# Sliding-window attention and a gated FFN on one Trainium2 core: batch 0 loaded and computed in two token halves, and every due time of the order set anew

## The chip, the cores and the metric

The kernel runs on one core of one Trainium2 chip. The metric is device time in microseconds (us), read as the median of several runs. The engines are PE (TensorE, matmul, with PEld for its weight loads), DVE (VectorE), ACT (ScalarE), POOL (GpSimd) and SP (SyncE, which here only issues transfers). SBUF is the on-chip memory of 128 partitions, PSUM the eight banks that PE writes to.

## The reference

Attention in 8 batches of 8 heads, 576 tokens, head dimension 64, each token looking 32 tokens to each side, then a feed-forward layer whose gate is a convolution over three tokens:

```python
scores = q @ k.T / 8                      # where |i - j| <= 32, else -1e9
attn = softmax(scores); x = attn @ v      # heads side by side: x is [8, 576, 512]
h = relu(x @ w_in)                        # [8, 576, 1024]
conv = conv_w[0] * h[t-1] + conv_w[1] * h[t] + conv_w[2] * h[t+1]   # per channel
out = (h * sigmoid(conv)) @ w_out         # [8, 576, 512]
```

All inputs are float32; the kernel casts to bfloat16 on the chip.

## The kernel before, in words

**Attention, per batch.** `loads(b)` brings in q and k in four transfers of 128 partitions (`qst`, `kst`: for each of q and k two groups of four heads; a partition holds 9 consecutive tokens of a head, 2304 bytes, for two pairs of heads) and v in five blocks of 128 tokens shifted by 32 (`vst`). POOL casts each to bfloat16 (`qb`, `kb`, `ve`). DVE makes a second copy of v shifted by 64 tokens (`vo`, `shift`). `transposes` (line 479) turns q and k on PE, ACT and DVE copy the result to `qT` and `kT`. `scores` (line 509) works on a pair of heads: PE multiplies 64 queries by the 128 keys around them, ACT takes the exponential in two parts (five and four query blocks), and DVE multiplies by the 0/1 `mask`. `values` (line 537) multiplies by `ve` and `vo`, whose 65th column of ones gives the sum; DVE takes its reciprocal (`rec`) and writes the normalised `xn`. `x_turned` (line 578) turns `xn` on PE, and ACT or DVE copy it to `xT`, the input of the FFN.

**FFN.** Two batches, 1152 tokens, make three chunks of 384 tokens, 12 chunks in all. `first` (line 615) multiplies by `w_in`, one of eight blocks m of 128 channels at a time, and ACT or DVE take the relu into `hT`. `gates` (line 705) does the convolution as 32x32 matmuls with diagonal weights (`diag_w`) for four blocks, ACT takes a tanh (`tn`), DVE forms the product (`gT`). Since the convolution's result comes out turned by 32 partitions per block, `moves` (line 688) turns `hT` the same way by transfers (`gT<-hT`), and the rows of w_out are loaded turned. `second` (line 758) multiplies by `w_out`, and the copy to `wst` is stored. Chunk 0 needs batch 0 alone, chunk 1 the end of batch 0 and the start of batch 1, so chunk 1 of the first two batches is done in two parts: part 0 is its half in batch 0, part 1 the one in batch 1. Chunk 2 lies in batch 1.

**Who sets the order.** Nothing is issued while the code above runs. Each step is a task with its engines, an estimated duration, what it reads and writes, and a due time t; `Order.run` (line 65) then plays a list schedule: at each step the engine that can start first takes, among its ready tasks, the one with the least t. The instructions are issued in the order found and each engine keeps to it, so an instruction that waits holds up everything behind it on its engine. The due times come from the numbers in `PARAMS` (line 832): start times of the chunks, the distance of the pairs, offsets for each kind of step. Loads of batches 0 and 1 are due long before time 0, in the order batch 0, w_in (two halves of 1 MB through `wst`), batch 1, w_out. All these transfers go through SP's one queue; a load waits until the casts have emptied its staging tile, and further until the queue has room. The staging tiles for q, k and v exist once; the cast tiles exist for two batches, the `attn` tiles for four pairs.

Lines of the profile: nearly all work is issued through a helper (line 274), so the rows below tell instructions by their tiles.

Of the kernel before, what the change touches and what calls it, by code (L numbers as in the profile page):

```python
# [31 lines left out]
class Order:  # L32
# [3 lines left out]
    def __init__(self):  # L36
        self.tasks, self.writer, self.readers = [], {}, {}

    def add(self, kinds, emit, t, reads=(), writes=(), opens=None, ps=(), after=(), claims=()):


        deps = set(after)
# [10 lines left out]
        task = Task(len(self.tasks), kinds, emit, t, deps, opens, ps)  # L53
        task.soft = soft - deps
        for k in reads:
            self.readers.setdefault(k, []).append(task)
# [8 lines left out]
    def run(self, emit=True):  # L65
        free = {"PE": 0.0, "ACT": 2800.0, "DVE": 6000.0, "POOL": 4400.0, "SP": 800.0}
# [128 lines left out]
def kernel(  # L195
# [152 lines left out]

    def loads(b):
        i = b % NLD  # L350

        def load_qk(y, j):
            src = (q, k)[y][b, 4 * j:4 * j + 4, :, :]
            sync.dma_start(
                qkst[y][j].rearrange("p e j d -> p e (j d)"),
                bass.AP(src.tensor, src.offset, [[RP * D, 128], [2 * S * D, 2], [1, RP * D]]),
            )

# [21 lines left out]
        if b < 2:  # L380
            x, dx = (-100.0 if b == 0 else -50.0), 0.1
        else:
            x, dx = t0 - PARAMS["LD"], Q["LX"]
# [5 lines left out]

        for j in range(NPH):  # L390
            for y in range(2):
                t = x + n * dx
                o.add({"SP": dma(256, 110)}, lambda e, y=y, j=j: load_qk(y, j), t,
                      writes=[("st", y, j)], after=paced())
                before.append(o.tasks[-1])
                o.add({"POOL": pl(1152)}, lambda e, y=y, j=j: cast_qk(y, j, e), t,
                      reads=[("st", y, j)], writes=[("b", i, y, j)])
                n += 1
        for c in range(NBLK):
            t = x + n * dx  # L400
            o.add({"SP": dma(1024, 21)}, lambda e, c=c: load_v(c), t, writes=[("vst", c)], after=paced())
            before.append(o.tasks[-1])
            o.add({"POOL": pl(512)}, lambda e, c=c: cast_v(c, e), t,
                  reads=[("vst", c)], writes=[("ve", i, c)])
            n += 1
        for cs in ((0, 2), (2, 4)) if b == 0 else ((0, 4),):
            for half in range(2):
                o.add({"DVE": dve(520 * (cs[1] - cs[0]), 4)},
                      lambda e, cs=cs, half=half: shift(half, cs), x + n * dx,
                      reads=[("ve", i, c + half) for c in range(*cs)],  # L410
                      writes=[("vo", i, c, half) for c in range(*cs)])

    def load_w_in():
        for h in range(2):
# [9 lines left out]
            o.add({"SP": dma(512, 95)}, load, -60.0, writes=[("ws", 4 * h + c) for c in range(4)])  # L424
            for c in range(KC):
                o.add({"POOL": pl(512)}, lambda e, h=h, c=c: cast(e, h, c), -60.0 + h,
                      reads=[("ws", 4 * h + c)], writes=[("w_in", h, c)])

    def load_w_out():
        rows = moe_w_out.rearrange("(h c p) f -> p h c f", c=4, p=128)  # L430
        for c in range(4):
            def load(e, c=c):
                for lo, at, n in turn(c):
# [5 lines left out]
            o.add({"SP": dma(256, 95, len(turn(c)))}, load, -40.0,  # L439
                  writes=[("ws", 4 * h + c) for h in range(2)])  # L440
            for h in range(2):
                o.add({"POOL": pl(512)}, lambda e, h=h, c=c: copy(e, w_out_sb[:, 4 * h + c, :], ws[:, 4 * h + c, :]),
# [18 lines left out]
    def conv_weights():  # L461
        ps = Banks(1)
        o.add({"PE": pe(200.0, "f32")},
              lambda e: tensor.matmul(bank(ps, 0)[:, 0:3 * MB], conv_w24, ident24, start=True, stop=True),
              5.0, opens=ps, writes=[("cw24",)])
        o.add({"DVE": dve(24)}, lambda e: vector.tensor_copy(
            out=conv_w_sb.rearrange("p k m -> p (k m)"), in_=bank(ps, 0)[:, 0:3 * MB]),
            5.0, reads=[("cw24",)], writes=[("cw",)], ps=[ps])
        o.add({"DVE": dve(768)}, lambda e: vector.tensor_tensor(
# [5 lines left out]
    def transposes(g2):  # L475
# [3 lines left out]
        i, n = b % NLD, g2 % NKT  # L479
        for y in range(2):  # L480
# [16 lines left out]
            o.add({"PE": pe(280.0, "rows")}, mm, t + Q["TR"],  # L497
                  reads=[("b", i, y, j)], writes=[("tr", g2, y)], opens=ps,
                  claims=[("T", n, y, h) for h in range(2)])
            for h in range(2):  # L500
                o.add({"ACT": act(576), "DVE": dve(576)},
                      lambda e, ps=ps, h=h, to=to: copy(
                          e, to[:, h, :, :], half(ps, h).rearrange("p (j x) -> p x j", x=64)),
                      t + Q["TC"], reads=[("tr", g2, y)], writes=[("T", n, y, h)], ps=[ps])
# [4 lines left out]
    def scores(g):  # L509
# [3 lines left out]
        for part, ts in enumerate((range(0, 5), range(5, 9))):  # L513
            ps = Banks(2, 2)
            w = 64 * len(ts)

            def mm(e, ps=ps, ts=ts):
                for x in ts:
# [8 lines left out]
            o.add({"PE": pe(28.0 * len(ts), "rows")}, mm, t + Q["SC"] * d,  # L527
                  reads=[("T", n, y_, y) for y_ in range(2)],
                  writes=[("sc", g, part)], opens=ps, claims=[("a", a, part)])
            o.add({"ACT": act(2 * w)},  # L530
# [3 lines left out]
                  t + Q["EX"] * d, reads=[("sc", g, part)], writes=[("a", a, part)], ps=[ps])  # L534
        o.add({"DVE": (850.0, 850.0, None)},
# [3 lines left out]
    def values(g):  # L539
# [5 lines left out]
        ps = Banks(2, 2)  # L545

        def mm(e):
            for h in range(2):
                for c in range(NBLK):
                    for j in range(2):  # L550
                        x = min(2 * c + j, NT - 1)
                        tensor.matmul(
                            bank(ps, h)[64 * j:64 * j + 64, 65 * c:65 * c + 65],
# [6 lines left out]
        o.add({"PE": pe(29.0 * 10, "cols")}, mm, t + Q["AV"] * d,  # L560
              reads=[("a", a, 0), ("a", a, 1)] + [("ve", i, c) for c in range(NBLK)]
              + [("vo", i, c, h) for c in range(NBLK - 1) for h in range(2)],
              writes=[("av", g)], opens=ps, claims=[("xn", b % 2, pr), ("rec", a)])

        def po():
            return pair(ps, 0)[:, :, 0:65 * NBLK].rearrange("p e (c x) -> p e c x", x=65)
# [301 lines left out]
```

## Time and profile before

| | us |
|---|---|
| median of 3 runs (lowest, highest) | 241.77 (241.15, 247.62) |
| the profiled execution's own time | 243.37 |
| its span in the trace | 241.7 |
| PE busy | 208.1 |
| ACT busy | 164.0 |
| DVE busy | 160.1 |
| POOL busy | 80.9 |

The span is what the trace covers, from the first instruction to the last; the profiled execution's time has 1.67 us more, which lie outside it. A row of the timeline gives start, length, engine, line, operation, destination and source tile with their shapes, how many instructions are merged in it, and in brackets how long the engine had been idle before and what ended that. The forty digits of a row of the page are slices of 6.04 us: busy share in tenths, or the granted clock of PE in tenths of full speed.

### The profile page before, as it was taken

Reading aid. Unit: us, or ns where it says so; the run is one execution under the profiler, and the core shown is the slowest. Engines: PE = TensorE matmul, PEld = TensorE weight load, DVE = VectorE, ACT = ScalarE, POOL = GpSimd, SP = SyncE. Lnnn points to the kernel's source line nnn. Section 1 sums busy time; section 2 is a strip of 40 time slices with the busy share of each in tenths; the row PEclk is TensorE's granted clock in tenths of the full one; section 3 lists DMA queues with packets and bytes.
Section 4 is the critical chain, followed back from the end, with each engine's and each line's share of the span. In section 5 each row is a group of like instructions: output and inputs, shape, how many; then the busy total and the mean of one; then the engine's idle time right before and its main releaser. Section 6 shows DMA issues by size and latency. Waiting matters only on the chain. (4 is left out here: it accounts for less than half of the span.)

```text
span 241.7 us, 9128 instructions
## 1 busy us (share of the span) xinstructions
PE 208.1 (86%) x3878; PEld 124.3 (51%) x3906; DVE 160.1 (66%) x268; ACT 164.0 (68%) x291; POOL 80.9 (33%) x96
## 2 busy tenths in 40 slices
PE   1536995589998869999999998999999999999993
PEld 0425464365655454565455654655555655555541
DVE  7586166998575899546399779698684595524140
ACT  1650586445698576679977886679778885876751
POOL 5757744536613444662236517321000000000000
PEclk9999999758999997999999999999999999999999
DMA  6999999989698899969489989756132223342534
GB/s 237 292 289 392 248 233 223 275 229 337 168 290 186 217 293 355 328 186 278 98 207 356 264 225 281 161 129 205 37 129 55 79 105 68 123 110 54 177 113 181
DMA packets 67228, 49.62 MB, mean 205 GB/s; under 512 B 46172, under 2 KB 52340, under 8 KB 67188
## 3 DMA queue, kind: packets, MB, share of 16 engines
q1 hardware_dynamic: 67152, 49.03, 71.6%
q8 instruction: 30, 0.49, 0.9%
q14 instruction: 10, 0.08, 0.1%
q10 hardware_dynamic: 36, 0.01, 0.0%
HBM read 32.52 MB, written 9.44 MB: 174 GB/s over the span
## 5 line engine op out<-in xcount | busy, mean ns | idle before, releaser
L274 PE MATMUL pst<-xT,w_in_sb 128*128 128x385 bf16 (+2 forms) x416 | 75.4, 322 | 1.6 <-ACT xT L274 0.6
L274 PE MATMUL pst<-w_out_sb,gT 128*128 128x512 bf16 x260 | 64.3, 384 | 3.2 <-issue 2.2
L274 PEld LDWEIGHTS <-w_in_sb 128*128 128x128 bf16 x416 | 37.6, 100 | 25.8 <-issue 3.4
L274 ACT ACTIVATE hT<-pst 128x385 bf16<-128x385 f32 (+2 forms) x80 | 38.6, 489 | 11.1 <-PE pst L274 10.1
L274 DVE SCALAR_TENSOR_TENSOR gT<-tn,gT 128x384 bf16<-128x384 f32 (+2 forms) x52 | 42.4, 842 | 3.9 <-DMA gT<-hT 3.9
L274 POOL CAST ve<-vst 128x512 bf16<-128x512 f32 x40 | 29.4, 741 | 45.7 <-DMA vst<-in_v_dram 43.5
L274 ACT ACTIVATE attn<-pst 128x640 bf16<-128x640 f32 x64 | 39.4, 667 | 4.9 <-PE pst L274 4.9
L274 PEld LDWEIGHTS <-gT 128*128 128x128 bf16 x288 | 26.6, 99 | 31.0 <-issue 3.3
L274 ACT ACTIVATE tn<-pst 128x768 f32<-128x768 f32 (+1 forms) x52 | 37.4, 768 | 6.5 <-PE pst L274 4.6
L274 ACT COPY wst<-pst 128x512 f32<-128x512 f32 x36 | 21.2, 588 | 29.6 <-PE pst L274 28.1
L274 DVE TENSOR_TENSOR attn<-attn,mask 128x1152 bf16<-128x1152 bf16 x32 | 26.9, 846 | 12.3 <-ACT attn L274 12.1
L274 DVE TENSOR_TENSOR xn<-pst,rec 128x640 bf16<-128x640 f32 x32 | 25.8, 818 | 0.5
L274 DVE SCALAR_TENSOR_TENSOR gT<-tn,hT 128x384 bf16<-128x384 f32 (+1 forms) x26 | 14.7, 564 | 16.5 <-ACT tn L274 16.4
L274 POOL CAST qb<-qst 128x1152 bf16<-128x1152 f32 x16 | 19.9, 1242 | 16.2 <-DMA qst<-in_q_dram 12.5
L274 POOL CAST kb<-kst 128x1152 bf16<-128x1152 f32 x16 | 19.9, 1243 | 16.0 <-DMA kst<-in_k_dram 14.3
L274 PE MATMUL pst<-hT,diag_w 32*32 32x384 bf16 (+1 forms) x1248 | 21.2, 322 | 1.8 <-DVE xn L274 1.0
L274 ACT COPY xT<-pst 128x1024 bf16<-128x1024 bf16 (+1 forms) x16 | 11.8, 781 | 13.9 <-PE pst L274 13.9
L274 PEld LDWEIGHTS <-attn 128*64 128x64 bf16 x640 | 14.1, 119 | 13.6 <-issue 8.6
L274 PE MATMUL pst<-ve,attn 128*64 128x65 bf16 x384 | 17.4, 206 | 3.8 <-DVE attn L274 2.3
L274 PE MATMUL pst<-qT,kT 64*128 64x64 bf16 x576 | 17.5, 197 | 3.1 <-DVE kT L274 0.8
L274 PE MATMUL pst<-vo,attn 128*64 128x65 bf16 x256 | 15.6, 206 | 3.3 <-DVE vo L274 3.3
L274 PEld LDWEIGHTS <-kT 64*128 64x128 bf16 x576 | 12.2, 98 | 12.0 <-issue 9.2
(37 smaller groups left out, 163.4 us busy)
## 6 DMA issues: line engine op xcount, KB each, us to landing
qst<-in_q_dram SPq DMA_DIRECT2D x16, 576.0 KB, 6.4
kst<-in_k_dram SPq DMA_DIRECT2D x16, 576.0 KB, 7.3
out_dram<-wst SPq DMA_DIRECT2D x11, 768.0 KB, 5.8
vst<-in_v_dram SPq DMA_DIRECT2D x24, 256.0 KB, 5.5
vst<-in_v_dram SPq DMA_DIRECT2D x16, 192.0 KB, 5.9
wst<-in_moe_w_in_dram SPq DMA_DIRECT2D x2, 1024.0 KB, 7.9
gT<-hT SPq DMA_DIRECT2D x14, 144.0 KB, 3.6
gT<-hT SPq DMA_DIRECT2D x34, 48.0 KB, 2.1
```

Source lines behind the costliest of these rows:

```text
L274: return lambda *args, **kwargs: fixed(do(*args, **kwargs))
```

## The change

Batch 0 is split in two halves by tokens in q and k (tokens 0 to 287 and 288 to 575). Each half load of q or k is two transfers of 64 partitions (32 rows by two heads, the rows outermost); the first halves of k are issued on ACT's queue, all others on SP's. Each half is cast, turned, scored, masked and multiplied with v by itself: the scores in query blocks 0 to 3 and 4 to 8, the values in token blocks 0, 1 and 2 to 4. Transposes of batch 0 are 64x64 in place of 64x128. `load_w_in` takes one half at a time and stands behind the half of batch 0; its casts may go to ACT as well as to POOL. All loads of batches 0 and 1, w_in and w_out are tied to one another in a line, in the order in which they are added. Chunk 0's `first` is done in two halves of 193 and 192 columns; its `gates`, `moves` and `second` are as before. Each task gets a name and an index, `NUDGE` adds an offset to its due time, and `PARAMS` has new values. Two estimates of the planner differ: ACT is counted free from 5400 ns on, not 2800, and the copy of `xT` on DVE at twice the rate. Batches 1 to 7 have the same instructions as before, in another order.

```diff
+    def add(self, name, kinds, emit, t, ..., claims=(), sub=0, line=None):
+        index = self.index + 20 * sub
+        t += self.nudge.get(name, {}).get(index, 0.0)
...
+        if line:
+            soft.add(line[-1])
+        if line is not None:
+            line.append(task)
...
-        free = {"PE": 0.0, "ACT": 2800.0, "DVE": 6000.0, "POOL": 4400.0, "SP": 800.0}
+        free = {"PE": 0.0, "ACT": 5400.0, "DVE": 6000.0, "POOL": 4400.0, "SP": 800.0}
...
+        def load_half(y, j, half):
+            for e_ in range(2):
+                src = (q, k)[y][b, 4 * j + 2 * e_:4 * j + 2 * e_ + 2, 32 * RP * half:32 * RP * half + 32 * RP, :]
+                (scalar if y and not half else sync).dma_start(
+                    qkst[y][j][64 * e_:64 * e_ + 64, half, :, :].rearrange("p j d -> p (j d)"),
+                    bass.AP(src.tensor, src.offset, [[RP * D, 32], [S * D, 2], [1, RP * D]]),
+                )
...
+        if b == 0:
+            for half in range(2):
+                t = x + 3.0 * half
+                for j in range(NPH):
+                    for y in range(2):
+                        o.add("qk", ..., load_half(y, j, half), t, writes=[("st0", y, j, half)], sub=half, line=lead)
+                        o.add("qc", {"POOL": pl(576)}, ..., cast_half(y, j, half, e), t, ...)
+                        t += 0.1
+                for c in (range(0, 3), range(3, NBLK))[half]:
+                    v_block(c, t)
+                    t += 0.1
+                v_shift((2 * half, 2 * half + 2), t)
+                load_w_in(half, t + 1.0)
+            return
...
-                o.add({"POOL": pl(512)}, lambda e, h=h, c=c: cast(e, h, c), -60.0 + h,
-                      reads=[("ws", 4 * h + c)], writes=[("w_in", h, c)])
+                o.add("wic", {"POOL": pl(512), "ACT": act(512)}, lambda e, h=h, c=c: cast(e, h, c), t,
+                      reads=[("ws", 4 * h + c)], writes=[("w_in", h, c)], sub=h)
...
+        if b == 0:
+            for half in range(2):
+                for y in range(2):
+                    transposes_half(g2, y, half, t + Q["B0"] * half)
+            return
...
-        for part, ts in enumerate((range(0, 5), range(5, 9))):
+        for part, ts in enumerate((range(0, 4), range(4, 9)) if first_ else (range(0, 5), range(5, 9))):
...
+            if first_:
+                lo = 64 * ts[0]
+                o.add("mk", ..., attn[:, :, lo:lo + w] * mask[:, :, lo:lo + w], ...)
...
+        cs = range(NBLK) if part is None else (range(0, 2), range(2, NBLK))[part]
...
+        if c == 0:
+            for m in range(MB):
+                first(c, m, 0, T0 + Q["A0"] + m * 0.5)
...
-                    first(c, m, part, t + m * dt)
+                    first(c, m, part if c else 1, t + m * dt)
...
-        for i in range(NP):
-            values(b * NP + i)
+        for part in (0, 1) if b == 0 else (None,):
+            for i in range(NP):
+                values(b * NP + i, part)
...
-PARAMS = {"P": 23.98, "T0": 17.65, "T1": 35.65, "T2": 7.73, "B1": 27.27, "LD": 15, "LEAD": 0,
-          "EARLY": 2.48, "MV": 2000.0, "C1": 8.2, "PY": 6, "TR": -5.1, "TC": -10, "SC": -0.08,
...
+PARAMS = {"P": 26.5, "T0": 10, "T1": 34.66, "T2": 16, "B1": 22.98, "LD": 21.05, "LEAD": 6.54,
+          "EARLY": 6.11, "MV": 2000.0, "C1": 7.98, "PY": 5.59, "TR": -1.75, "TC": -7.8,
...
+NUDGE = {
+    "qk": {0: 50.82, 1: -13.88, 2: 12.29, 3: -10.82, 4: 21.55, 5: 73.01, 6: 1.84, 7: 16.51,
+        20: 21.78},
...
```

More of the change, by code (lines that the diff above doesn't have):

```diff
@@ L380, in loads @@
         if b < 2:
[L381 removed]
+            x, dx = -100.0, 0.1
         else:
@@ L525, in mm @@
                         )
[L527 to L530, printed above, removed]
+            o.add("sc", {"PE": pe(28.0 * len(ts), "rows")}, mm, t + Q["SC"] * d,
+                  reads=need, writes=[("sc", g, part)], opens=ps, claims=into,
+                  sub=part if first_ else 0)
+            o.add("ex", {"ACT": act(2 * w)},
                   lambda e, ps=ps, ts=ts, w=w: scalar.activation(
```

216 lines of the change are left out of this document (144 added, 72 removed), and 72 rows, old and new, of tables (NUDGE, PARAMS).

## Prediction

> **What bounds the kernel now.** I read the page first: the span, the busy times, the forty slices.
>
> ```profile
> span 241.7 us, 9128 instructions
> ...
> PE 208.1 (86%) x3878; PEld 124.3 (51%) x3906; DVE 160.1 (66%) x268; ACT 164.0 (68%) x291; POOL 80.9 (33%) x96
> PE   1536995589998869999999998999999999999993
> ...
> PEclk9999999758999997999999999999999999999999
> ```
>
> TensorE (PE) carries the kernel: 208.1 us of 241.7, so 33.6 us idle, most of it in the first ten slices of 6 us. Next I asked for the busy times by stage. The columns behind the window are its length, then busy us of PE, PEld, DVE, ACT and POOL, granted clock, share of the DMA engines and GB/s.
>
> ```profile
> 0.00:12.00 12.00, 4.09 (x110) 3.59 (x110) 7.91 (x26) 4.91 (x8) 7.64 (x13) 1.00 0.93 265
> 12.00:25.50 13.50, 6.74 (x142) 5.24 (x136) 9.84 (x18) 4.67 (x8) 9.76 (x15) 1.00 1.07 344
> 25.50:36.00 10.50, 10.46 (x183) 6.31 (x184) 3.70 (x8) 7.05 (x13) 5.88 (x8) 1.00 0.99 223
> 36.00:49.80 13.80, 7.33 (x228) 5.58 (x205) 11.48 (x21) 6.83 (x13) 6.67 (x9) 0.84 0.94 236
> 49.80:55.60 5.80, 5.80 (x125) 4.07 (x126) 4.99 (x10) 3.66 (x6) 2.48 (x3) 0.50 0.93 289
> 55.60:70.00 14.40, 13.88 (x285) 8.65 (x286) 10.73 (x16) 10.03 (x22) 7.88 (x8) 1.00 0.87 252
> 70.00:90.00 20.00, 16.09 (x400) 10.09 (x401) 16.38 (x26) 15.73 (x28) 7.82 (x10) 0.99 0.92 236
> ...
> 96.00:230.00 134.00, 130.24 (x2333) 74.13 (x2352) 86.96 (x139) 103.09 (x184) 30.36 (x32) 1.00 0.59 166
> 230.00:241.70 11.70, 7.82 (x81) 3.52 (x80) 2.24 (x4) 4.44 (x7) 0.00 (x0) 1.00 0.40 148
> ```
>
> Three stretches matter. To 25.5 PE lacks 14.7 us while the DMA engines are full (0.93, 1.07). From 36 to 49.8 it lacks 6.5 us, and after that it is full but at half clock: 5.8 us that do the work of 2.9. From 70 to 90 it lacks 3.9 us. From 96 to 230 only 3.8 us of 134 are idle, and the 3.9 us after 230 are the tail of the last rows. So the time is set by when PE gets its full supply, and that is when batch 1's attention has been turned: chunks 2 and up need it. The timeline shows the stations to that point (start, length, engine, operation, and the wait before it).
>
> ```profile
> 4.76 1.14 POOL L274 CAST qb<-qst 128x1152 bf16<-128x1152 f32 x1 [1.65 <-DMA qst<-in_q_dram]
> ...
> 10.15 1.15 POOL L274 CAST kb<-kst 128x1152 bf16<-128x1152 f32 x1 [0.78 <-DMA kst<-in_k_dram]
> ...
> 15.14 0.79 POOL L274 CAST ve<-vst 128x512 bf16<-128x512 f32 x1 [0.47 <-DMA vst<-in_v_dram]
> 16.49 0.99 POOL L274 CAST ve<-vst 128x512 bf16<-128x512 f32 x1 [0.56 <-DMA vst<-in_v_dram]
> 18.90 2.29 POOL L274 CAST w_in_sb<-wst 128x512 bf16<-128x512 f32 x4 [1.43 <-DMA wst<-in_moe_w_in_dram]
> 21.63 2.29 POOL L274 CAST w_in_sb<-wst 128x512 bf16<-128x512 f32 x4 [0.44 <-DMA wst<-in_moe_w_in_dram]
> 23.86 1.15 POOL L274 CAST qb<-qst 128x1152 bf16<-128x1152 f32 x1
> ...
> 28.58 1.15 POOL L274 CAST kb<-kst 128x1152 bf16<-128x1152 f32 x1 [0.81 <-DMA kst<-in_k_dram]
> ...
> 34.57 0.62 POOL L274 CAST ve<-vst 128x512 bf16<-128x512 f32 x1 [1.53 <-DMA vst<-in_v_dram]
> ```
>
> POOL waits for a DMA before nearly every cast: the loads set the pace. Batch 0's four q and k loads arrive 1.8 us apart ((10.15 − 4.76) / 3), a block of v every 1.35 us, half of w_in in 2.73 us. The last block of batch 1's v is cast at 35.2.
>
> ```profile
> 36.11 0.76 DVE L274 TENSOR_TENSOR attn<-attn,mask 128x1152 bf16<-128x1152 bf16 x1
> 36.85 0.76 DVE L274 COPY qT<-pst 128x576 bf16<-128x576 bf16 x1
> 39.45 0.76 DVE L274 COPY kT<-pst 128x576 bf16<-128x576 bf16 x1 [1.84 <-PE pst L274]
> 40.23 1.03 DVE L274 COPY vo<-ve 64x2080 bf16<-64x2080 bf16 x1
> ...
> 42.16 1.11 DVE L274 COPY vo<-ve 64x2080 bf16<-64x2080 bf16 x1
> ...
> 44.28 0.21 DVE L274 RECIPROCAL rec<-pst 128x10 f32<-128x10 f32 x1
> ...
> 48.90 0.82 DVE L274 TENSOR_TENSOR xn<-pst,rec 128x640 bf16<-128x640 f32 x1
> ```
>
> Though v was there at 35.2, VectorE (DVE) shifts it only at 40.23: it stands behind a copy of kT, which waits for PE. The shift ends at 43.27, the last xn at 49.72. **This chain of 14.5 us behind the last load is what I expect to shrink.**
>
> **The change part by part.**
>
> *Loads.* The same bytes in another order: half 0 of q and k, v blocks 0 to 2, half of w_in, then the second halves, then batch 1. By the rates above: the first halves of q and k are in at about 6.5 (3.6 us for four half loads, the first some 0.9 us sooner than 4.76), v 0 to 2 at 10.3, w_in's first half at 13.0, the second halves at 16.6, v 3 and 4 at 19.3, the rest of w_in at 22.0. That was 21.63, so batch 1 comes as before and its last v at about 35. Eight more issues on SP at 0.46 us (12 in place of 4) cost nothing while the queue is full. Four go to ACT, at the 0.65 us of its own first one (row below): 0.80 + 5 × 0.65 = 4.05, before ACT's table load at 5.07. A 64-partition load has no row; its rate lies between the 295 KB in 0.9 us taken here and half of that, which would add 7.2 us for all four and both halves; I take no loss, since the nearest rows, the 128-partition loads, move the same pieces of 2304 bytes. With the whole 7.2 the sum below would come to 241.
>
> ```profile
> 0.80 0.65 ACTq L305 DMA_DIRECT2D conv_w<-in_moe_conv_w_dram  x1
> ...
> 0.80 0.44 SPq L274 DMA_DIRECT2D qst<-in_q_dram  x1
> ...
> 1.30 0.46 SPq L274 DMA_DIRECT2D kst<-in_k_dram  x1
> ...
> 5.07 1.28 ACT L274 ACT_TABLE_LOAD   x1 [5.07 <-DVE conv_w_sb L274]
> ...
> 5.96 0.66 PE L274 MATMUL pst<-ident,qb 64*128 64x64 bf16 x18 [2.14 <-POOL qb L274]
> ```
>
> The Trainium skill (Perfetto Trace Analysis, DMA Optimizations) says splitting transfers lets some start sooner if the DMA engines are generally idle. Here they are not (0.93, 1.07), and by that rule the split brings nothing: the time would be the first rival's below.
>
> *Added work in batch 0.* PE: 72 more transposes at 0.66 / 18 us, 2.6 us; DVE: four masks, four reciprocals, four xn more. A half costs more than half: relu takes 0.56 us for 385 columns and 0.36 for 193 (rows below), so 0.16 is fixed, and 12 × 0.16 = 1.9 us. Chunk 0's relus, 16 in place of 8, add 8 × 0.16 = 1.3 on ACT and DVE. POOL's casts add about 4 × 0.1. All of it falls before 25.5, where PE has 6.8 us free from 12 on, DVE 3.7, ACT 8.8, POOL 3.7: costed at 0. If that cover were gone, DVE's 1.9 would be paid; that is the other end.
>
> ```profile
> 32.67 0.56 DVE L274 TENSOR_SCALAR hT<-pst 128x385 bf16<-128x385 f32 x1 [1.08 <-ACT tn L274]
> ...
> 34.64 0.36 DVE L274 TENSOR_SCALAR hT<-pst 128x193 bf16<-128x193 f32 x1 [0.68 <-PE pst L274]
> ```
>
> *Chunk 0's first half earlier.* Its input needs only tokens 0 to 255 and w_in's first half, so four of its eight blocks can run from about 16 on, all eight from about 23. Until now its first weight load came at 25.51, and PE was then full to 36 (10.46 us of 10.5), so batch 1's transposes and scores were mixed in late and DVE waited for the kT copy till 39.45. Weight loads of that stretch show the pace:
>
> ```profile
> 25.51 0.14 PEld L274 LDWEIGHTS <-w_in_sb 128*128 128x128 bf16 x2 [0.68 <-POOL qb L274]
> ...
> 27.74 0.15 PEld L274 LDWEIGHTS <-w_in_sb 128*128 128x128 bf16 x1 [0.17 <-issue]
> 28.06 1.20 PEld L274 LDWEIGHTS <-w_in_sb 128*128 128x128 bf16 x7 [0.17 <-issue]
> ```
>
> One per 0.32 us up to 28.06, then about 0.16: PE is at half speed until then, though the granted clock reads 1.00. Half of chunk 0 is 32 matmuls, 5.1 us at half speed, that leave the full stretch for the idle one.
>
> *Batch 1's chain.* With 5.1 us off PE and w_in's casts allowed on ACT too (POOL's last four, 2.29 us, are what the cast at 23.86 follows without a wait), the transposes of batch 1 can be copied before v is in. Then the shift starts at 35.2, ends after 1.03 + 1.11 at 37.3, and the chain of the four pairs follows. Before, that took 49.72 − 43.27 = 6.45 with three masks in it; without them four times (0.21 + 0.82) = 4.1. So the last xn ends between 41.4 and 43.8, 8.3 to 5.9 us earlier. No gain is the other bound, if DVE is again busy with something else. I take the cautious row, 5.9, call it 6: what is late next is DVE, with chunk 0's products. PE has 6.5 us idle there to absorb the shift.
>
> *Clock after 45.* Half clock from 49.8 to 55.6 costs 2.9 us. The stretch before will again be a thin one, so I count 0; −2.9 is the bound.
>
> *New targets everywhere.* Every priority is another, so every later wait can go or grow. What can go: 0.5 + 3.9 + 3.8 idle after 55.6 without the tail, 8.2. What can come: the gap of 70 to 90 once more, 3.9. Between −8.2 and +3.9 the middle is −2.2; I take −2.
>
> **Sum.** 241.7 − 6 − 2 = 233.7 us of span. The profiled execution took 243.37 us, 1.67 beyond its span; the median of the runs is 241.77, 1.60 below it, as long as the span. In the runs' measure: 241.77 − 8 = **233.8 us**.
>
> **The rivals.**
>
> *Nothing moves (241).* The loads end as before, DVE is in demand from 36 to 49.8 (11.48 of 13.8), and half 1 of batch 0 is later by 2.8 us (v at 19.3 for 16.49). If DVE takes products and masks ahead of the shift, the 14.5 us stay. Price: the start gains 0, and the later part keeps between nothing and half of its 2: 241. For it: the full DMA. Against: v lay there unused for 5 us. With what the targets may do, between 238 and 244. The Trainium skill's rule on splitting (Perfetto Trace Analysis, DMA Optimizations) ends in this case.
>
> *PE stays fed (227).* The last xn at 41.4 (−8.3), no half clock (−2.9) and −3.5 of the later idle: 241.8 − 14.7 = 227.1. For it: idle DVE from 25.5 to 36 (3.70 of 10.5). Against: the loads still leave PE little to do till 35.
>
> *Slower (248).* DVE becomes the bound from 70 to 96. It is busy 16.38 of 20 there, and batch 3's shift, masks and xn go through it while PE waits. If the targets put products before them, as they did in 36 to 49.8, each pair adds a mask and a wait, and PE drops to half clock. It decides when the new idle time there passes the 8 us gained; 5 us more, and the kernel is slower by over 2%. Price: a second gap like 36 to 55.6 (6.5 + 2.9) and batch 1's gain lost, less 3 us of the rest: 241.8 + 9.4 − 3 = 248. Against: PE is at 97% from 96 on, under the same priority rule.
>
> **How the numbers follow.** About 2% is what measurement can tell from no change: below 236.9 is faster, above 246.6 slower. Forecast 0.58, for which I give 229 to 237; PE fed 0.12; nothing moves 0.20; slower 0.10. Faster 0.70, same 0.20, slower 0.10. The range goes from the fed case to the top of the unmoved one: 227 to 243; outside lie the slower case and bits of two others.
>
> **What would show it.** Right: a matmul of chunk 0 with 193 columns before 22; the last v cast of batch 1 near 35; the shift of v within a us of it; the last xn of batch 1 by 44; PE full from 45 on. Wrong: v's last cast after 38 (the half loads are slow); the shift late again (DVE order); more than 8 us of idle PE between 55 and 96 (targets); relus or masks of batch 0 still running at 26 (the added work was not covered).

## The result, and the profile after

The kernel before took 241.67 us (median, 241.15 to 247.62), the changed one 250.23 us (247.15 to 250.98): a ratio of 1.032, with a 95% interval of 1.022 to 1.041. It is slower, where the forecast was 3% faster, and it lies outside the forecast's range. The profile shown is of a run of 247.15 us, and that of before of one of 243.37, so of the 8.6 us between the medians they can show only the part that their spans have, 245.4 − 241.7 = 3.7 us. Here and below medians are over all runs of a kernel and ratios over its runs in the faster of the chip's two states, so the two need not agree.

First the page of the changed kernel (span, busy times, TensorE's slices of 6.1 us, granted clock), then its busy times in the windows shown of before.

```profile
span 245.4 us, 9371 instructions
...
PE 209.9 (86%) x3984; PEld 128.8 (52%) x4010; DVE 163.8 (67%) x289; ACT 159.8 (65%) x294; POOL 79.5 (32%) x96
PE   1658787357998978989999799999999999999994
...
PEclk9999799655999999999999999999999999999999
```

```profile
0.00:12.00 12.00, 4.31 (x106) 3.61 (x106) 4.95 (x24) 4.91 (x8) 6.89 (x15) 1.00 0.92 201
12.00:25.50 13.50, 8.52 (x196) 6.77 (x192) 8.53 (x22) 7.87 (x16) 6.26 (x11) 1.00 1.09 314
25.50:36.00 10.50, 9.23 (x133) 8.07 (x134) 4.69 (x14) 6.26 (x16) 7.38 (x9) 0.84 1.04 262
36.00:49.80 13.80, 7.62 (x246) 5.82 (x243) 8.06 (x14) 8.74 (x16) 7.04 (x11) 0.81 1.05 278
49.80:55.60 5.80, 3.16 (x116) 2.52 (x117) 5.43 (x10) 1.60 (x4) 3.32 (x3) 0.50 0.85 228
55.60:70.00 14.40, 12.93 (x206) 8.22 (x207) 9.16 (x17) 6.77 (x16) 7.62 (x8) 0.79 0.71 212
...
96.00:230.00 134.00, 129.55 (x2334) 74.50 (x2353) 100.71 (x156) 96.55 (x175) 33.15 (x34) 1.00 0.65 173
230.00:245.40 15.40, 11.71 (x98) 5.15 (x97) 3.37 (x6) 5.87 (x10) 0.00 (x0) 1.00 0.44 164
```

To 25.5 us PE is busy 2.0 us longer than before (4.31 + 8.52 against 4.09 + 6.74). From 25.5 to 49.8 it is busy 0.9 us less (9.23 + 7.62 against 10.46 + 7.33). Behind 96 the rows are alike: 129.55 of 134 against 130.24, and a tail with 3.7 us idle against 3.9. The largest difference lies at 48 to 60, of which these are the rows, first of before, then of after with the 12 us ahead of it:

```profile
48.00:60.00 12.00, 11.05 (x203) 7.20 (x204) 11.03 (x18) 5.79 (x11) 6.26 (x6) 0.68 0.94 279
```

```profile
36.00:48.00 12.00, 6.17 (x214) 4.80 (x213) 6.26 (x12) 7.46 (x14) 6.59 (x10) 0.85 1.06 270
48.00:60.00 12.00, 7.60 (x213) 5.28 (x215) 11.63 (x20) 4.75 (x9) 6.54 (x5) 0.50 0.95 286
```

I call lost time a window's idle PE time plus its busy time multiplied by one minus the clock. Before, these 12 us lose 0.95 + 11.05 × 0.32 = 4.5; after, 4.4 + 7.60 × 0.50 = 8.2. The difference, 3.7 us, is as large as that of the spans. The other windows differ too, but come to about nothing together: the changed kernel loses 2.0 us less to 25.5, 2.7 more from 25.5 to 36 and 2.4 less from 72 to 96. From 48 to 60 PE is at half clock and waits, while DVE is busy 11.63 of 12.

Two timelines of the changed kernel show what came late: first batch 0's second half and chunk 0, then batch 1.

```profile
5.38 1.14 POOL L283 CAST qb<-qst 128x576 bf16<-128x576 f32 x1 [2.27 <-DMA qst<-in_q_dram]
...
16.77 0.67 POOL L283 CAST qb<-qst 128x576 bf16<-128x576 f32 x1 [0.98 <-DMA qst<-in_q_dram]
...
18.44 2.50 PE L283 MATMUL pst<-xT,w_in_sb 128*128 128x193 bf16 x16 [0.17 <-DVE xT L283]
...
20.11 0.67 POOL L283 CAST kb<-kst 128x576 bf16<-128x576 f32 x1 [0.48 <-DMA kst<-in_k_dram]
...
24.20 2.12 DVE L283 TENSOR_TENSOR attn<-attn,mask 128x640 bf16<-128x640 bf16 x3
...
27.04 1.44 DVE L283 TENSOR_TENSOR xn<-pst,rec 128x384 bf16<-128x384 f32 x3
...
31.04 0.69 DVE L283 COPY xT<-pst 128x1024 bf16<-128x1024 bf16 x1 [1.89 <-PE pst L283]
31.79 1.42 PE L283 MATMUL pst<-xT,w_in_sb 128*128 128x193 bf16 x15 [0.41 <-DVE xT L283]
```

```profile
36.55 0.62 POOL L283 CAST ve<-vst 128x512 bf16<-128x512 f32 x1 [0.29 <-DMA vst<-in_v_dram]
...
40.83 1.12 DVE L283 COPY vo<-ve 64x2080 bf16<-64x2080 bf16 x1
...
46.55 0.50 PE L283 MATMUL pst<-ident,kb 64*128 64x64 bf16 x12 [3.91 <-issue]
47.13 0.76 DVE L283 COPY kT<-pst 128x576 bf16<-128x576 bf16 x1 [3.56 <-PE pst L283]
...
54.04 1.01 DVE L283 SCALAR_TENSOR_TENSOR gT<-tn,gT 128x384 bf16<-128x384 f32 x2
55.10 0.75 DVE L283 TENSOR_TENSOR xn<-pst,rec 128x640 bf16<-128x640 f32 x1
55.78 1.95 DVE L283 SCALAR_TENSOR_TENSOR gT<-tn,gT 128x768 bf16<-128x768 f32 x2
57.66 0.81 DVE L283 TENSOR_TENSOR xn<-pst,rec 128x640 bf16<-128x640 f32 x1
```

Chunk 0's first matmuls start at 18.44, as intended. But the second half's last cast of k starts at 20.11, and from there transposes, scores, exponentials, four masks, values, four xn and a turn follow one another until its x is copied at 31.73. Before, all of batch 0 had been turned and chunk 0 had begun at 25.51; now chunk 0's second half, mixed with chunk 1's part in batch 0, runs from 31.79 to 38.7. Batch 1's last k of the second group is then copied only from 47.13, behind a stop of PE, and its xn stand between chunk 0's products. The last xn ends at 58.47; before, 49.72; forecast, 43.8.

The ends of DVE's last copies of xT for batches 1, 2 and 3 are the stations I use from here on (ACT's last copies end at most 0.4 us later). Before:

```profile
54.25 0.28 DVE L274 COPY xT<-pst 128x256 bf16<-128x256 bf16 x1
93.20 0.28 DVE L274 COPY xT<-pst 128x256 bf16<-128x256 bf16 x1
107.16 0.69 DVE L274 COPY xT<-pst 128x1024 bf16<-128x1024 bf16 x1 [2.08 <-PE pst L274]
```

After:

```profile
62.35 1.46 DVE L283 COPY xT<-pst 128x1024 bf16<-128x1024 bf16 x2 [0.71 <-PE pst L283]
95.49 1.27 DVE L283 COPY xT<-pst 128x1024 bf16<-128x1024 bf16 x2
111.77 1.29 DVE L283 COPY xT<-pst 128x1024 bf16<-128x1024 bf16 x2 [1.97 <-PE pst L283]
```

That is 54.5, 93.5 and 107.9 against 63.8, 96.8 and 113.1: 9.3, 3.3 and 5.2 us later, and 3.7 later at the end.

### The profile page after: what moved, and what is told of

It is laid out like the page before. It is cut to its first block, busy times and chain, and to the rows that moved or that the text cites. A ratio compares the mean times of both kernels' runs of the same rounds, so it can differ in the third digit from the quotient of the medians.

```text
span 245.4 us, 9371 instructions
## 1 busy us (share of the span) xinstructions
PE 209.9 (86%) x3984; PEld 128.8 (52%) x4010; DVE 163.8 (67%) x289; ACT 159.8 (65%) x294; POOL 79.5 (32%) x96
## 4 chain that ended last, share of the span: by engine, by line
PE 58%; DMA 14%; DVE 11%; ACT 7%; issue 4%; SPq 2%; POOL 1%; ACTq 0%; DVEq 0%; POOLq 0%
PE pst L283 58%; DMA kst<-in_k_dram 5%; ACT attn L283 4%; DMA wst<-in_moe_w_out_dram 3%; DVE gT L283 3%; DVE xn L283 3%; DMA vst<-in_v_dram 3%; DMA qst<-in_q_dram 2%; DVE attn L283 2%; DMA gT<-hT 2%; SPq L283 2%; ACT tn L283 1%; DVE vo L283 1%; DVE hT L283 1%; ACT hT L283 1%
## 5 line engine op out<-in xcount | busy, mean ns | idle before, releaser
L283 PE MATMUL pst<-xT,w_in_sb 128*128 128x385 bf16 (+3 forms) x448 | 73.7, 312 | 1.4 <-DVE xT L283 0.7
L283 PEld LDWEIGHTS <-w_in_sb 128*128 128x128 bf16 x448 | 40.8, 100 | 22.4 <-issue 2.8
L283 ACT ACTIVATE hT<-pst 128x385 bf16<-128x385 f32 (+3 forms) x88 | 39.4, 462 | 13.8 <-PE pst L283 13.0
L283 ACT ACTIVATE attn<-pst 128x640 bf16<-128x640 f32 (+1 forms) x64 | 38.8, 662 | 5.6 <-PE pst L283 5.2
L283 DVE TENSOR_TENSOR attn<-attn,mask 128x1152 bf16<-128x1152 bf16 (+2 forms) x36 | 29.8, 835 | 11.2 <-ACT attn L283 10.7
L283 POOL CAST qb<-qst 128x1152 bf16<-128x1152 f32 (+1 forms) x18 | 20.8, 1157 | 26.1 <-DMA qst<-in_q_dram 22.4
L283 DVE TENSOR_SCALAR hT<-pst 128x385 bf16<-128x385 f32 (+3 forms) x24 | 11.6, 485 | 24.8 <-PE pst L283 16.6
L283 POOL CAST kb<-kst 128x1152 bf16<-128x1152 f32 (+1 forms) x18 | 19.2, 1068 | 23.4 <-DMA kst<-in_k_dram 15.2
L283 DVE TENSOR_TENSOR xn<-pst,rec 128x640 bf16<-128x640 f32 (+2 forms) x36 | 26.1, 738 | 0.5
L283 PEld LDWEIGHTS <-attn 128*64 128x64 bf16 x640 | 14.1, 119 | 16.4 <-issue 9.5
L283 ACT COPY qT<-pst 128x576 bf16<-128x576 bf16 x23 | 14.6, 655 | 7.6 <-PE pst L283 7.6
```

What stands on the lines that cost most here:

```text
L283: return lambda *args, **kwargs: fixed(do(*args, **kwargs))
```

## The experiments

**What they have to tell apart.** Theory A: the split itself, with half 1's chain of eleven us, makes the start late. Theory B: the new due times do it, and the split would have paid with the old ones. Theory C: the half loads are slow, or their queue is. Theory D: the loss is not in the start but in the order behind it. All ratios are to the kernel before, run on the same chip, with 95% intervals.

**The change's halves one at a time.** `targets_alone` loads and computes batch 0 whole and keeps the new due times and the planner's estimates. `split_old_targets` keeps the split with the old due times.

```diff
-        if b == 0:
+        if b == 0 and SPLIT:
...
+SPLIT = False
```

> Batch 0 and chunk 0 whole as before, loads and w_in in the order of before, w_in's casts on POOL alone; due times, offsets and planner estimates of the changed kernel. Theory H (batch 0's second half comes late, and all behind it): about as before, 239 to 243, the first block of batch 0's x turned near 21.5 and all of it by 25. Theory T (the new due times make an order that the chip runs badly): 247 or more, with the last xn of batch 1 after 55 as in the changed kernel.

Measured: 250.39 us, 1.024 (1.010 to 1.037). The due times alone cost 2.4%, without any split and with the old transfers; the forecast had them at −2 us. Batch 0's x is turned by 26.1 here (25 expected, 25.4 before), but batch 1's only by 59.5 (54.5 before).

```diff
-PARAMS = {"P": 26.5, "T0": 10, "T1": 34.66, "T2": 16, "B1": 22.98, "LD": 21.05, "LEAD": 6.54,
+PARAMS = {"P": 23.98, "T0": 17.65, "T1": 35.65, "T2": 7.73, "B1": 27.27, "LD": 15, "LEAD": 0,
...
-NUDGE = {
...
+NUDGE = {}
```

> The split in halves and the load order of the change, with the due times of before and no offsets. Theory H: still slow, 245 to 250, the last block of batch 0's x turned near 31 as in the changed kernel. Theory T: 242 or less, the last xn of batch 1 before 52.

Measured: 246.96 us (242.02 to 249.52) beside 243.17 (240.72 to 245.32) of the kernel before, with no usable interval. No gain shows with the old due times either, but whether there is a loss can't be read from this run; `halves_old_start` below asks again.

**The loads.** `w_in_behind` puts both halves of w_in behind batch 0's second half; `no_w_out_load` is the changed kernel, in its order, without the 2 MB of w_out.

```diff
-                load_w_in(half, t + 1.0)
+            for half in range(2):
+                load_w_in(half, x + 3.0 * half + (1.7 if half == 0 else 1.6))
```

> The changed kernel with one edit: both halves of w_in load behind batch 0's second half, not one between. Theory H: the last cast of batch 0's k comes 2.7 us earlier (near 18, not 20.1), x is turned 2 to 3 us earlier, and the time falls by 2 to 4 us to about 246. Theory T: no change beyond 1.5 us, unless the order happens to come out otherwise.

Measured: 261.86 us, 1.081 (1.071 to 1.091). The second half of k was cast from 17.61, 2.5 us sooner than in the changed kernel, but x was turned only by 30.2 and the last xn came at 59.2. It settles nothing: with other loads the planner put the whole kernel into another order, so the 8% can't be laid to the loads.

```diff
-                for lo, at, n in turn(c):
+                for lo, at, n in ():
```

> The changed kernel with w_out never loaded (its casts take what lies in the staging tile, so the second matmul uses other weights); the order of instructions is the same. Theory S (the 3.9 us in which PE stands in the midst of a row of transposes is an instruction fetch that waits behind full DMA engines, and the half clock follows from it): the stop at 42.6 shrinks below 1 us and the time falls by 4 to 7 us. Theory H: the stop may go, but the time falls by 2 us at most, since batch 0's half sets the start.

Measured: 246.35 us, 1.011 (0.999 to 1.023), two points less than the change. PE's stop is gone, and from 36 to 48 PE does 8.99 us where it did 6.17 in the changed kernel:

```profile
36.00:48.00 12.00, 8.99 (x283) 7.30 (x280) 8.19 (x15) 10.78 (x22) 7.11 (x11) 0.93 0.57 162
```

The same edit in the kernel before (`before_no_w_out`) tells whose cost it is.

> The kernel before without the load of w_out (its casts take what lies in the staging tile). The order is unchanged. If PE's stop of 2.2 us at 37 is a fetch behind full DMA engines, it goes here too, and the time falls by 2 to 4 us, near what no_w_out_load gained on the change (2.1 points): then the stop is no cost of the change by itself. If the time falls by under 1 us, the longer stop is a cost of the change.

Measured: 240.29 us, 0.993 (0.989 to 0.997). Without the load the change is still slower, 1.011 against 0.993, by 1.8%. The other 1.4 points of its 3.2% would then be that load's. This is an estimate: the interval of 1.011 alone goes from 0.999 to 1.023, and without the load not only the stop is gone, the DMA engines have less to do as well (a share of 0.57 from 36 to 48, in place of 1.06).

`whole_loads` brings both halves of q and k with the first transfers, in the order of the changed kernel; `whole_b1` is that with batch 1 put first as below; `k_on_sp` takes the k halves off ACT's queue.

```diff
-            for e_ in range(2):
-                src = (q, k)[y][b, 4 * j + 2 * e_:4 * j + 2 * e_ + 2, 32 * RP * half:32 * RP * half + 32 * RP, :]
+            for e_ in range(0 if half else 2):
+                src = (q, k)[y][b, 4 * j + 2 * e_:4 * j + 2 * e_ + 2, :, :]
```

> The changed kernel with the same order of instructions, but each first-half transfer of q and k brings both halves (64 partitions, two pieces of 2304 bytes each) and the second-half transfers are gone. Theory H: batch 0's second half is cast by 13, its x turned by 25 in place of 31, and the time falls by 4 us or more. Theory D: batch 0 may be earlier, but batch 1's last xn stays after 54 and the time falls by 2 us at most.

Measured: 254.56 us, 1.047 (1.038 to 1.056), and `whole_b1` 257.41 us, 1.061 (1.055 to 1.067). POOL keeps its order, so the second half's casts still wait behind v and w_in while everything else comes later: a miss, which says only that the kept order is made for the half loads.

```diff
-                (scalar if y and not half else sync).dma_start(
+                sync.dma_start(
```

> The changed kernel, its order unchanged, with the first halves of k issued on SP like all others. If ACT's queue slows the first loads (four q halves took SP 2.86 us, 0.72 each, where 0.46 was the rule): the first casts come 0.5 to 1 us earlier and the time falls by up to 2 us. If the queue does not matter: no change within 1.5 us, perhaps slower by the issues that SP now makes in a row.

Measured: 250.69 us, 1.034 (1.026 to 1.042): the queue makes no difference to the time. The first cast does come sooner (4.51 for 5.38), and batch 1's last v is cast 3.3 us later than in the changed kernel (by 40.51 for 37.17); in this order that costs nothing the runs can show.

**Batch 1 first.** If the end hangs on batch 1, its steps have only to be put ahead of all others. `b1_first` does that in the changed kernel, `before_b1_first` in the one before.

```diff
+for _n in ("tr", "tc", "sc", "ex", "mk", "av", "rc", "xm", "xt", "xc"):
+    for _i in ((1, 21, 41) if _n in ("xt", "xc") else (1,)):
+        NUDGE[_n][_i] = -100.0
```

> The changed kernel with one edit: batch 1's transposes, copies, scores, exponents, masks, values, xn and its turning get an offset of -100 us, so that each engine takes them before anything else that is ready. Theory D (the new due times let DVE do gate products and relus between batch 1's four pairs, so x of batch 1 comes late): the last xn of batch 1 ends by 50 in place of 58.5, PE is full from about 52, and the time falls by 5 us or more, to 245 or less. Theory H (batch 0's second half comes late): the last xn moves by 3 us at most, and the time stays above 247.

> The kernel before with the offset of -100 us on the same steps of batch 1, nothing of the split. Theory D: in the kernel before the chain stood behind other work too (the shift of v 5 us late), so the last xn moves from 49.7 to 46 or less and the time falls by up to 3 us, to 239. Theory H says nothing of it: 240 to 244.

Measured: 254.07 us, 1.045 (1.034 to 1.055), and 244.4 us, 1.009 (1.003 to 1.014). In both the last xn of batch 1 came sooner (52.9 and 47.2 us, against 58.47 and 49.72), and neither is faster than the kernel that it was made from. That was the first sign against the forecast's premise. But both were ordered anew to the end.

**Start and rest apart.** So in the next kernels each step is given the place that it has in another kernel's plan: the steps of batches 0 and 1 and chunks 0 to 2 ("start") from one kernel, all later ones ("rest") from another. The list schedule still decides ties and delays, so of the 230 pairs of neighbouring steps on PE in the rest 14 to 43 are other ones than in the plan that the rest is taken from (53 and 55 in `halves_whole_loads` and `b1_first_old_rest`, below).

```diff
+            if x.key in RANK:
+                e, x.t = RANK[x.key]
+                x.kinds = {e: x.kinds[e]}
```

> The changed kernel's start (loads and attention of batches 0 and 1, weights, chunks 0 to 2) in its order, and from batch 2 and chunk 3 on the order of the kernel before: each step is given the engine and the planned time that it had there as its due time. Theory S (the loss is made in the start): 247 to 250, as slow as the change. Theory R (the order of the rest is at fault): 242 to 244, about as before.

> The split in halves, with the due times and estimates of before in the start too; the rest in the order of before. It tells the split from the new due times. Theory S with the split at fault (batch 0's second half late): 245 or more, the last xn of batch 1 after 53. Theory S with the due times at fault: 243 or less, the last xn by 51.

> Batch 0 whole as before, the start ordered by the new due times, the rest in the order of before. Theory S with the due times at fault: 246 or more. Theory S with the split at fault, or theory R: 244 or less.

> The kernel before in its own order up to batch 1 and chunk 2, and the order of the changed kernel from batch 2 and chunk 3 on. Theory R: 246 or more. Theory S: 240 to 243, and where the rest of the new order is better, as its planner counts, 238.

| start | due times in it | rest | us | ratio (95%) |
|---|---|---|---|---|
| halves | new | old | 251.12 | 1.038 (1.031 to 1.045) |
| halves | old | old | 249.23 | 1.022 (1.014 to 1.029) |
| whole | new | old | 253.48 | 1.044 (1.038 to 1.051) |
| whole | old | new | 243.82 | 1.007 (1.003 to 1.011) |

D falls: the new rest behind the old start costs 0.7%. A, taken as the split together with its loads, and B are both right: each by itself is enough (2.2% and 4.4%), and they don't add.

`halves_whole_loads` keeps the halves in the computation, with old due times and old rest, but loads each q and k of batch 0 whole, with v and then w_in behind them, in the order of before. One thing is not as before: the transfers are still pairs of 64 partitions, where the kernel before has one of 128.

```diff
-                        o.add("qk", ..., t, writes=[("st0", y, j, half)], sub=half, line=lead)
+                        if not half:
+                            o.add("qk", ..., t, writes=[("st0", y, j, h) for h in range(2)], sub=half, line=lead)
```

> Batch 0 computed in halves, with due times and estimates of before, but loaded as before: each of q and k whole, both halves in one pair of transfers, then v, then w_in; the rest in the order of before (from batch 2 and chunk 3 on). To be held against halves_old_start (1.0215). If the transfers in halves and their order are what the split costs: 244 or less, x of batch 0 turned by 26. If computing in halves costs: 247 or more.

Measured: 250.31 us, 1.037 (1.031 to 1.042). x of batch 0 is turned by 30.8 (25.4 before). But its loads are slower than the old ones:

```profile
6.08 1.28 POOL L290 CAST qb<-qst 128x576 bf16<-128x576 f32 x2 [2.96 <-DMA qst<-in_q_dram]
...
13.81 1.68 POOL L290 CAST kb<-kst 128x576 bf16<-128x576 f32 x2 [1.31 <-DMA kst<-in_k_dram]
...
38.29 0.62 POOL L290 CAST ve<-vst 128x512 bf16<-128x512 f32 x1 [0.21 <-DMA vst<-in_v_dram]
```

They come 2.6 us apart ((13.81 − 6.08) / 3), where the same bytes in one transfer of 128 partitions came 1.8 us apart. So batch 0's last k is cast from 13.81 in place of 10.15, and batch 1's last v by 38.91 in place of 35.19. What falls is the idea that the order in which the halves are loaded makes the loss. C itself doesn't fall: no run computes batch 0 in halves on loads of 128 partitions, so A and C are not told apart.

**Does an earlier start pay at all?** `b1_first_old_rest` is the kernel before with batch 1 first in the start and the old rest behind it.

> The kernel before, with batch 1's steps first in the start and the rest (batch 2, chunk 3 and on) in the order of before. The start alone gained some 5 us of PE time up to 60 us in before_b1_first. If the start sets the end, as the prediction had it: 237 to 239. If the rest is bound by something else (loads, DVE), the gain is lost again: 241 to 244.

Measured: 244.54 us, 1.014 (1.008 to 1.019). The profile is of a run of 246.51 us, 2.0 above the median, with a span of 244.8. Its stations:

```profile
48.00 0.69 DVE L290 COPY xT<-pst 128x1024 bf16<-128x1024 bf16 x1 [0.60 <-PE pst L290]
...
91.93 0.28 DVE L290 COPY xT<-pst 128x256 bf16<-128x256 bf16 x1
...
106.68 0.69 DVE L290 COPY xT<-pst 128x1024 bf16<-128x1024 bf16 x1 [1.56 <-PE pst L290]
```

Four of its windows, then one of the kernel before:

```profile
48.00:60.00 12.00, 11.23 (x242) 6.85 (x242) 9.54 (x15) 9.23 (x22) 4.71 (x5) 1.00 0.85 262
...
72.00:96.00 24.00, 19.63 (x396) 12.44 (x396) 18.17 (x27) 17.17 (x30) 10.22 (x12) 0.79 0.93 250
...
140.00:146.00 6.00, 4.24 (x102) 2.27 (x101) 4.08 (x7) 4.00 (x7) 1.61 (x2) 1.00 1.08 244
146.00:150.00 4.00, 4.00 (x55) 2.23 (x56) 2.61 (x4) 1.58 (x3) 2.84 (x3) 0.57 0.83 239
```

```profile
72.00:96.00 24.00, 20.09 (x373) 12.10 (x376) 20.53 (x31) 17.37 (x30) 9.62 (x12) 0.93 0.95 262
```

48.7, 92.2 and 107.4: batch 1 is 5.8 us earlier than before, batch 3 by 0.5. From 48 to 60 PE loses 0.8 us here (4.5 before). It is at full clock to 72 and then loses 4.4 + 19.63 × 0.21 = 8.5 us by 96, where the kernel before lost 3.9 + 20.09 × 0.07 = 5.3. Much of the start's gain is handed back there, with the DMA engines at 0.93 (before 0.95).

That explains why nothing is gained, not why the kernel is slower: from batch 3's station to the end of the span it takes 137.4 us, before 133.8. Of these 3.6 us about 2.6 lie from 140 to 150, where PE loses 1.8 + 4.00 × 0.43 = 3.5 (0.9 before). The rest is not quite in the order of before, so this part may be the order's.

Theory L says that the loads of batches 2 and 3 take the gain; rival P, that the engines' own work does. The last pair takes these loads away in both orders (the casts find old data).

```diff
         def load_qk(y, j):
+            if b in (2, 3):
+                return
...
         def load_v(c):
+            if b in (2, 3):
+                return
```

> The kernel before, in its own order, without the loads of q, k and v of batches 2 and 3: their casts read what batches 0 and 1 left in the staging tiles, so those two batches compute with other data. It leaves out 18 of the 72 loads (q and k 8, v 10), 7 of some 28 MB of inputs, all of them issued between about 42 and 110 us. Theory L (the stretch from 55 to 107 goes at the pace of these loads, which come on SP's one queue between the moves of hT to gT): batch 3's x is turned well before 107.9, by 104 or sooner, and the time falls by 1.5 to 3% below the kernel before. Rival P (PE's own work is the limit there, and the loads lie beside it): batch 3's x at 107 to 108.5, the time within 0.7%.

> The kernel with batch 1 put first in the start and the old order behind it (b1_first_old_rest, which was 1.0136 of the kernel before), in that order, and without the same loads of batches 2 and 3. Its start turns batch 1's x some 3 us sooner and by 60 us had lost 6.8 us less, yet batch 3's x was turned at 107.6 as against 107.9. Theory L: the loads of batches 2 and 3 gave that gain back; without them it stays, this kernel turns batch 3's x 2 us or more ahead of before_no_23 and is faster than it by 1% or more, where with the loads it was slower by 1.4%. Rival P: the gain goes in any case, in DVE's and ACT's work of 72 to 96 us; this kernel is again 0.5 to 2% slower than before_no_23.

Measured: 244.93 us, 1.003 (0.997 to 1.009), and 239.91 us, 0.989 (0.984 to 0.993). Their stations, in the same order:

```profile
59.20 0.27 DVE L274 COPY xT<-pst 128x256 bf16<-128x256 bf16 x1
95.33 0.28 DVE L274 COPY xT<-pst 128x256 bf16<-128x256 bf16 x1
109.41 0.69 DVE L274 COPY xT<-pst 128x1024 bf16<-128x1024 bf16 x1 [2.08 <-PE pst L274]
```

```profile
49.01 0.69 DVE L290 COPY xT<-pst 128x1024 bf16<-128x1024 bf16 x1 [0.45 <-PE pst L290]
...
88.52 0.29 DVE L290 COPY xT<-pst 128x256 bf16<-128x256 bf16 x1 [0.23 <-PE pst L290]
...
103.50 0.69 DVE L290 COPY xT<-pst 128x1024 bf16<-128x1024 bf16 x1 [1.56 <-PE pst L290]
```

The sign turns, as theory L had it: with these loads the earlier start is 1.4% slower than the kernel before, without them 1.4% faster than its counterpart (0.989 to 1.003). Its batch 3 is then 5.9 us ahead (104.2 to 110.1). Theory L's first number missed, though: taking the loads from the kernel before brings nothing. Its batch 1 came 4.9 us later than with them (59.5 for 54.5), behind a stop of PE of 4.08 us that lasts 2.17 in the kernel before (last section). So a later start may hide what the loads gave back, and the pair is not a clean comparison of the start alone. What holds is narrower: the loads of batches 2 and 3 are one thing that takes an earlier start's gain away.

No run that does all the work was faster than the kernel before.

## Why the prediction was wrong, step by step

*What bounds the kernel.* "So the time is set by when PE gets its full supply, and that is when batch 1's attention has been turned": as a price for an earlier start this premise failed. In `b1_first_old_rest` batch 1 is turned 5.8 us sooner, batch 3 only 0.5 us sooner, and the kernel is 1.4% slower. A later start does cost (9.3 us at batch 1 in the changed kernel, 5.2 at batch 3); an earlier one didn't pay here, in part because of the loads of batches 2 and 3. The rows of 70 to 90 with DMA at 0.92 stood in the forecast; I read them as DVE's bound and only as a rival.

*Loads, the 64 partitions at no loss.* **The first step of the sum that failed.** To 12 us the DMA engines were as busy as before (0.92 and 0.93) and moved 201 GB/s in place of 265. The first cast starts at 5.38 (forecast 3.9), the last one of q's first half waits for its transfer until 8.15 (forecast 6.5), and the second halves came 1.11 us apart ((20.11 − 16.77) / 3) where I took 0.9. So the last k of the second half is cast from 20.11, 3.5 us behind the 16.6 of the forecast, and the last v of batch 1 by 37.17, 2.0 us late. The bound of 7.2 us that I had left at 0 was used by half at that k. The Trainium skill (Perfetto Trace Analysis, DMA Optimizations) says that a split may let some transfers start sooner, and the whole end sooner if the DMA engines are generally idle. They were at 0.92 and above, and the trace agrees: the first halves were all cast by 9.4 (11.3 before), the whole came later. How much of the 3.2% is the slow loads' stays open: `k_on_sp` shows that 3.3 us more at batch 1's v cost the changed order nothing, but batch 0's second half hangs on them.

*Added work in batch 0, costed at 0.* **The second step that failed.** I added up what each engine has free before 25.5 and asked whether the work fits. It would have fitted; it isn't free to move. The second half's work can only begin when its k is in (20.11 + 0.67), and behind that stands a chain of ten steps across PE, ACT and DVE that took 11.0 us to the turned x at 31.73. In the kernel before, the way from the last k (10.15 + 1.15) to the turned x (25.39) was even longer, 14.1 us with a wait for v in it, so a chain of that kind stood in the trace. With the forecast's own 16.6 for the last k, eleven us behind it end at 28.2, 2.8 us late; the slow loads add the other 3.5 to make the 6.3 us on batch 0's x. The end I named for a missing cover, 1.9 us of DVE, was the cost of throughput, and the cost was in latency. Masks of batch 0 still ran at 26 (24.20 + 2.12), one of the signs that I had named.

*Chunk 0's first half earlier.* It started at 18.44, before 22 as forecast. Nothing came of it: half of chunk 0 left the full stretch, and the other half moved from 25.5 back, with chunk 1's part, to 31.8 to 38.7, into the time of batch 1's transposes and scores.

*Batch 1's chain, −6.* Measured +8.8 (58.47 for 49.72). The shift of v was not within a us of the last cast but at 40.83; kT was copied at 47.13, behind a stop of PE; and chunk 0's products at 54.04 and 55.78 stand between the last three xn, where before they came behind them. One reading of the kernel before was wrong as well: I put the kT copy's wait till 39.45 down to a full PE, but PE stood still from 37.05 to 39.22, 16 transposes into that row of 18 (last section). The targets couldn't take that wait away, and in the changed kernel it was longer.

*Clock after 45, 0.* Half clock lasts from 44.4 to 61.5 us in place of 45.4 to 55.6. I expected a thin stretch ahead of it as before, and it was one: PE was busy 7.62 of 13.8 us, before 7.33. What failed is the stretch behind it: before, PE was busy without a break from 49.8 to 55.6 and then had its clock back; here it was busy 3.16 of these 5.8 us.

*New targets, −2.* **The third step that failed.** Measured +2.4%, some 6 us, for all of them without the split (`targets_alone`); in the start alone +4.4%, in the rest alone +0.7%. I took the middle of what could go and what could come, which is no estimate where the order of everything changes.

*Rivals.* "Slower" had the right sign and nearly the right size (248 for 250) by another mechanism: I placed a DVE-bound stretch with products ahead of a batch's chain at 70 to 96, batch 3; it came at 48 to 60, batch 1. The row of 70 to 90 is better than before (18.04 us busy of 20 for 16.09):

```profile
70.00:90.00 20.00, 18.04 (x420) 10.46 (x421) 12.90 (x22) 16.47 (x30) 6.07 (x8) 1.00 0.91 222
```

**What stays open.** Whether the split would pay, or at least not lose, on loads as fast as the old ones was not run, and why a pair of 64-partition transfers is slower isn't known. Of half 1's ten steps only one wait is plain: the last xn ends at 28.48 and its turn begins at 30.03, behind matmuls of chunk 0's first half. Why the new due times alone make the start late isn't known beyond their stations (`whole_new_start` turns batch 1's x by 61.8). And the earlier start's loss from 72 to 96 is only partly the loads': without them 3.7 + 20.30 × 0.07 = 5.1 us are still lost there.

```profile
72.00:96.00 24.00, 20.30 (x428) 13.01 (x423) 20.23 (x29) 19.06 (x34) 16.39 (x15) 0.93 0.91 281
```

## What to carry to other kernels

Before costing added work at nothing because engines are idle, draw its chain from the last input that it needs: idle time before that input arrives can't take it, and what counts is when its last link lets the next stage begin. Before pricing an earlier station at its full lead, look for the next arrival that the stage behind it waits for; an earlier start is worth no more than that leaves, while a later one costs. A transfer of a new shape has no price until a row shows one: here the same bytes took 2.6 us in place of 1.8, and the far bound belonged in the sum. In a kernel ordered by a list schedule, test an edit with the rest of the order held, since an edit and a new order are two changes.

## What the runs showed of the hardware

*Loads.* The 576 KB of a group of q or k came 1.8 us apart as one transfer of 128 partitions (kernel before) and 2.6 us apart as two of 64 in the same order (`halves_whole_loads`).

*A stop of PE.* PE stops in the middle of a row of transposes, with nothing that it waits for in the trace. The stop comes at one and the same transpose of a given order: 2.17 us in the kernel before, 4.08 in the same order without the loads of batches 2 and 3 (row below), 3.91 in the changed kernel, 4.11 at the same transpose in `k_on_sp`, and no such stop in the two runs without the load of w_out (nor in every order with it: `targets_alone` has none there). The trace also has a DMA queue named `q8 instruction`; in the kernel before it moves 30 packets of 16 KB, 0.49 MB, about 63 bytes for each of PE's 7784 matmuls and weight loads. In all four kernels one of these packets ends within the stop, at 37.9, 40.8, 45.0 and 46.7 us in the order above, and PE goes on 1.4 to 1.6 us behind it. So PE most likely waits there for its next instructions. That their fetch was late because it stood behind transfers is argued, not shown: the DMA share was 1.02 in the stop of 2.17 us and 1.03 in that of 4.08.

```profile
42.41 0.24 PE L274 MATMUL pst<-ident,kb 64*128 64x64 bf16 x2 [4.08 <-issue]
```
